# Seven half-size products of the last layer: one PSUM tile per output block, K blocks in pairs, one operand change issued later

## The chip, the cores and the metric

One core of one Trainium2 chip runs the whole program. The metric is the device time of one execution in microseconds, median over the runs. TensorE (PE) multiplies and writes only to PSUM; VectorE (DVE), ScalarE (ACT) and GpSimd (POOL) prepare its operands and read its results; SyncE (SP) issues nearly all DMAs.

## The reference

Attention over 12 heads and two batches of 448 tokens (scores capped with tanh, softmax, times v), then a gated MLP with a token-mixing matrix, then a token-mixing MLP and a channel MLP:

```python
    xt = x.transpose(0, 2, 1)
    h = np.maximum(xt @ w_tok1, 0.0) @ w_tok2
    u = x + h.transpose(0, 2, 1)
    h2 = np.maximum(u @ w_ch1, 0.0) @ w_ch2
    return (u + h2).astype(np.float32)
```

The change touches the last product alone: `relu(...) @ w_ch2`, with 1536 inner channels, 768 output channels and 2 x 448 tokens, and the sum with `u` that follows it.

## The kernel before, in words

Every product takes its two operands as a high part (fp32r) and a rest, and adds three matmuls per K block of 128: high x high, high x rest, rest x high (`three`). The high part is a cast (line 417 on ACT, 422 on POOL), the rest a subtraction (line 434 on DVE, 435 on POOL).

The program is not emitted in the order in which it is written. Each step becomes an `Op` with a key (a wish for its place), dependencies, buffers and one or more engines that may run it, each with a modelled duration and a handicap in ns. `Plan.schedule` is a list scheduler: it repeatedly takes the operation that can start first, the lower key in a tie, and writes out one fixed order per engine. Buffers are tiles with a tag and a fixed number per tag (`BUFS`): 20 of `a`, 13 of `h`, 6 of `v`, `q` and `x`, 3 of `t`; in PSUM four of `gm` (one bank each) and two of `sc` (two banks each). A `Part` is a view of a tile that the planner follows as a buffer of its own; the tile is given back when all its parts are done. `DVE` and `POOL` work on SBUF alone shares a modelled port.

The last layer, `ch2_all`, is done with seven products of half-size blocks in place of eight (a 2 x 2 scheme in which sums and differences of blocks are multiplied). Rows of the weight halves are `a11, a12, a21, a22`, the token halves `b11, b12, b21, b22`, each in six K blocks `j`. The phases, in the order of PE:

- phase 0: a11 b11 into banks `x`; copied by ACT to `part` (line 1206); phase 1 adds a12 b21 onto it, giving output rows 0 to 2 of batch 0
- phase 2: (a22 - a11 + a21) (b22 - b12 + b11) into banks `y`, in the code `s2` and `t2`
- phase 3: the changed a11 times the changed b12 into banks `z`; read by DVE to `part[3 + i]` (line 1185); phase 4 adds a22 times the changed b21 onto it
- phase 5: the changed a21 times the changed b11 into banks `v`; read by DVE onto `U`; phase 6 adds the changed a12 times b22

A phase has three output blocks `i` of 128 channels, hence 6 x 3 steps of three matmuls (`product`, line 1168 issues them). The order is set by `step`: before, in phases 0 to 5 for each `j` the blocks 0, 1, 2 one after the other; in phase 6 all `j` of block 0, then of block 1, then of block 2. `banks` hands out the three accumulators of a phase: blocks 0 and 1 are the two halves of one `sc` tile, block 2 is a `gm` tile; in phases 5 and 6 the third is `last_bank`, which lives past the end.

The operands of a step (`weight`, `tokens`) take a fresh `a` tile each. The six changes of a K block (lines 1216 to 1224) are one DVE or POOL operation each (line 1105 on DVE, 1106 on POOL): four make `s2` and `t2`, the others change a12, b21, b12 and a21 in place. `t2` and `s2` are tiles of tag `t`. `combine` with `LATE_ON` adds intermediate results to `U` outside the products. The kernel ends with a branch, the last addition (line 1383) and two stores.

Of the kernel before, what the change touches and what calls it, by code (L numbers as in the profile page):

```python
# [13 lines left out]
ALU = mybir.AluOpType  # L14
PSUM = bass.MemoryType.PSUM

B, H, S, D = 2, 12, 448, 64
# [14 lines left out]
KH = NC // 2  # L32
# [13 lines left out]
WARM = 6  # L46
ANY = {"ACT": 0, "DVE": 0, "POOL": 0}
CAST, REST_ON = ANY, {"DVE": 0}
SUM_ON, LATE_ON, HI_ON = {"DVE": 0, "POOL": 300}, {"DVE": 300, "POOL": 0}, {"ACT": 0, "POOL": 300, "DVE": 600}
ON = {  # L50
    "TH": {"ACT": 300, "POOL": 0},
    "TL": {"DVE": 0, "POOL": 0},
# [215 lines left out]
class Net:  # L268
# [841 lines left out]
    def ch2_all(self, hr, kept, k, ask):  # L1110
# [5 lines left out]

        nc, io = self.nc, self.io
        key = lambda phase, j, lead=0.0: k + (KH * phase + j) * 1.72 - lead
        step = lambda phase, j, i: key(6, (j + KH * i) / 3) if phase == 6 else key(phase, j) + 0.1 * i
        whole = [self.buf("x", [128, 4, S]) for _ in range(KH)]  # L1120
        pairs = [self.a([128, 2, 384]) for _ in range(KH // 2)]
        rows = lambda i: [Part(x, lambda ap: ap[:, i]) for x in whole]
        a11 = [self.buf("v", [128, 384]) for _ in range(KH)]
        a12 = [Part(pairs[j // 2], lambda ap, j=j: ap[:, j % 2]) for j in range(KH)]
        a21, a22 = ([self.h([128, 384]) for _ in range(KH)] for _ in range(2))
        part = rows(0)
        U = [rows(1), rows(2)]
        for b in range(B):
            for d in range(ND):
# [6 lines left out]
                    key=key((2, 5, 3, 4)[2 * b + d // 3], 0, 20) + 0.1 * d,  # L1136
                )
        b11, b12 = ([hr[j][b] for j in range(KH)] for b in range(B))
        b21, b22 = ([hr[KH + j][b] for j in range(KH)] for b in range(B))
# [6 lines left out]
        def weight(t, at):  # L1146
            w = self.a([128, 2, 384], F32R)
            self.split(384, lambda: w[:, 0], lambda: w[:, 1], lambda: t.ap, [t], [w], at, HI_ON, SUM_ON)
            return w

        def tokens(t, at):
            w = self.a([128, 2, S], F32R)
            self.split(S, lambda: w[:, 0], lambda: w[:, 1], lambda: t.ap, [t], [w], at, HI_ON, SUM_ON)
            return w

        def change(out, a, b, op, n, at):
            self.combine(n, lambda: out.ap, lambda: a.ap, lambda: b.ap, op, [a, b], [out], at, SUM_ON)

        def product(phase, banks, j, a, b, more=False):
            for i in range(3):  # L1160
                terms = self.three(
                    lambda m, i=i: a[:, m, i * 128 : (i + 1) * 128], lambda m: b[:, m], [a, b]
                )

                def fn(i=i, terms=terms):
                    for n, (term, _) in enumerate(terms):
                        l, r = term()
                        nc.tensor.matmul(  # L1168
                            banks[i].ap[:, :S],
                            l,  # L1170
                            r,
                            start=not more and (j, n) == (0, 0),
                            stop=(j, n) == (KH - 1, 2),
                            skip_group_check=more,
                        )

                self.pe(3, fn, [a, b], [banks[i]], step(phase, j, i))

        def banks(last=None):
            two = self.bank2()  # L1180
            return [Part(two, lambda ap, i=i: ap[:, i]) for i in range(2)] + [last or self.bank()]

        def onto(out, bank, other, at, size=S):
            return self.dve(
                S, lambda: nc.vector.tensor_tensor(out=out.ap, in0=bank.ap[:, :S], in1=other.ap, op=ALU.add), [bank, other], [out], key=at  # L1185
            )
# [11 lines left out]
        for j in js:  # L1198
            for n, (t, row, col) in enumerate(((a11[j], 0, 0), (a21[j], 0, 1), (a22[j], 1, 1), (a12[j], 1, 0))):
                narrow(t, row, col, j, k - AHEAD + (4 * j + n) * PACE)  # L1200
        x = banks()
        for j in js:
            product(0, x, j, weight(a11[j], key(0, j, 9)), tokens(b11[j], key(0, j, 8)))
        for i in three:
            t = part[i]
# [3 lines left out]
        for i in three:  # L1209
            z = U[0][i]  # L1210
            onto(z, x[i], z, key(2, 0))
            store(z, i, 0, key(2, 1))
        y = banks()
        for j in js:
            s2, t2 = self.buf("t", [128, 384]), self.buf("t", [128, S])
            change(a11[j], a11[j], a21[j], ALU.subtract, 384, key(2, j, 16))
            change(s2, a22[j], a11[j], ALU.subtract, 384, key(2, j, 15))
            change(b11[j], b12[j], b11[j], ALU.subtract, S, key(2, j, 16))
            change(t2, b22[j], b11[j], ALU.subtract, S, key(2, j, 15))
            product(2, y, j, weight(s2, key(2, j, 9)), tokens(t2, key(2, j, 8)))  # L1220
            change(a12[j], a12[j], s2, ALU.subtract, 384, key(2, j, 7))
            change(b21[j], b21[j], t2, ALU.subtract, S, key(2, j, 7))
            change(b12[j], b22[j], b12[j], ALU.subtract, S, key(3, j, 14))
            change(a21[j], a21[j], a22[j], ALU.add, 384, key(5, j, 14))
        for i in three:
# [10 lines left out]
        for i in three:  # L1236
# [5 lines left out]
                S, lambda u=u: u.ap, lambda u=u: u.ap, lambda i=i: part[3 + i].ap, ALU.add, [u, part[3 + i]], [u], key(5, 2), LATE_ON  # L1242
# [21 lines left out]
        for i in three:  # L1264
            u = U[1][3 + i]
            last = onto(u, v[i], u, key(6, 0, 4))
# [188 lines left out]
```

## Time and profile before

| | us |
|---|---|
| median of 3 runs | 407.14 (407.09 to 408.88) |
| the profiled execution's own time | 407.99 |
| its span, first to last instruction | 406.1 |
| PE busy | 393.4 (97%) |
| DVE busy | 303.3 (75%) |
| ACT busy | 275.5 (68%) |
| POOL busy | 70.2 (17%) |

The last layer's products run from 319.1 us to the end. Busy shares are averages over stages of different kinds; the stage that the change touches has to be read by itself. A busy PE in such a table includes matmuls that overlap, so the start-to-start distance of steps shows its pace better.

### The profile page before, as it was taken

The numbers are of one execution on the slowest core, as the hardware profiler recorded it, in microseconds if no ns is written. First come the engines' busy times: TensorE is split into PE (matmuls) and PEld (weight loads), VectorE is DVE, ScalarE is ACT, GpSimd is POOL, SyncE is SP. The second block draws the span as 40 slices with busy tenths as digits, with TensorE's granted clock in tenths as the row PEclk, the third lists the DMA queues.
The fourth block names the chain that finished last, engine by engine and source line by source line (L and its number), as shares of the span: only waits on it lengthen the run. The fifth ranks groups of instructions, "written<-read, shape, count | busy, mean of one in ns | idle before, by whom it ended". The sixth has DMA issues, their size and how long they took to land. (4 is left out here: it accounts for less than half of the span.)

```text
span 406.1 us, 5812 instructions
## 1 busy us (share of the span) xinstructions
PE 393.4 (97%) x2102; PEld 302.3 (74%) x2102; DVE 303.3 (75%) x523; ACT 275.5 (68%) x443; POOL 70.2 (17%) x71
## 2 busy tenths in 40 slices
PE   8999989999999999999999999999999999998985
PEld 4222225565558899999999998899898989988974
DVE  1799999998467869975389964255984679999941
ACT  5999999999683587364268866767978445454510
POOL 1112130100002416671001110000000011750100
PEclk9999999999999999999999999999999999999999
DMA  7965343434001014043006755545564610100121
GB/s 236 392 268 196 92 163 121 162 119 157 0 2 51 1 56 140 2 155 103 2 1 218 241 190 183 168 169 180 147 187 148 222 53 0 69 1 2 69 85 59
DMA packets 19189, 48.79 MB, mean 120 GB/s; under 512 B 2384, under 2 KB 7888, under 8 KB 19152
## 3 DMA queue, kind: packets, MB, share of 16 engines
q1 hardware_dynamic: 19008, 48.23, 35.9%
q8 instruction: 18, 0.29, 0.3%
q14 instruction: 19, 0.16, 0.1%
q10 hardware_dynamic: 144, 0.11, 0.1%
HBM read 42.83 MB, written 5.51 MB: 119 GB/s over the span
## 5 line engine op out<-in xcount | busy, mean ns | idle before, releaser
L330 PE MATMUL sc<-x,a 128*128 128x384 f32 (+2 forms) x432 | 87.7, 364 | 0.0
L330 PEld LDWEIGHTS sc<-x,a 128*128 128x128 f32 x432 | 78.8, 188 | 8.8
L1168 PE MATMUL sc<-a,a 128*128 128x448 f32 x252 | 58.1, 368 | 3.9 <-DVE x L1185 3.4
L1168 PEld LDWEIGHTS sc<-a,a 128*128 128x128 f32 x252 | 47.0, 188 | 9.5 <-ACT a L417 2.3
L472 ACT ACTIVATE r<-r 128x512 f32<-128x512 f32 (+2 forms) x64 | 40.6, 639 | 11.5 <-DMA r<-ch_in 10.7
L330 PE MATMUL gm<-a,a 128*128 128x448 f32 (+1 forms) x232 | 46.3, 356 | 0.0
L330 PEld LDWEIGHTS gm<-a,a 128*128 128x128 f32 x232 | 42.0, 188 | 2.2
L585 ACT ACTIVATE a<-a,acap 128x896 f32<-128x896 f32 x42 | 43.2, 1075 | 0.1
L576 ACT ACTIVATE a<-sc,qs 128x896 f32<-128x896 f32 x42 | 41.5, 1035 | 1.9 <-DVE a L667 0.8
L506 DVE SCALAR_TENSOR_TENSOR t<-r,t 128x512 int32<-128x512 int32 (+1 forms) x34 | 25.4, 754 | 21.9 <-ACT t L498 20.1
L435 POOL TENSOR_TENSOR a<-t,a 128x512 fp32r<-128x512 f32 x12 | 18.9, 1575 | 99.4 <-DVE a L418 78.2
L330 PE MATMUL gm<-q,a 128*128 128x448 f32 x160 | 33.0, 366 | 0.0
L605 PE MATMUL sc<-q 64*64 64x448 f32 x264 | 30.1, 553 | 2.3 <-ACT a L576 2.3
L330 PEld LDWEIGHTS gm<-q,a 128*128 128x128 f32 x160 | 30.0, 188 | 2.6
L1168 PE MATMUL gm<-a,a 128*128 128x448 f32 x126 | 31.8, 367 | 0.0
L631 PE MATMUL gm<-a,v 128*64 128x448 f32 x144 | 30.9, 548 | 0.0
L330 PE MATMUL gm<-x,a 128*128 128x448 f32 x144 | 30.5, 368 | 0.0
L330 PEld LDWEIGHTS gm<-x,a 128*128 128x128 f32 x144 | 26.7, 188 | 4.9 <-DVE v L418 1.4
L484 ACT ACTIVATE t<-r 128x512 uint16<-128x512 uint16 (+1 forms) x34 | 27.1, 801 | 2.9 <-DVE a L434 2.0
L656 DVE TENSOR_TENSOR a<-a,a 128x896 f32<-128x896 f32 (+1 forms) x24 | 26.9, 1122 | 1.9 <-ACT a L585 1.6
L498 ACT ACTIVATE t<-r 128x512 f16<-128x512 f32 (+1 forms) x34 | 27.0, 799 | 0.0
L330 PE MATMUL gm<-a,x 128*128 128x512 f32 x108 | 26.5, 397 | 0.0
(128 smaller groups left out, 577.8 us busy)
## 6 DMA issues: line engine op xcount, KB each, us to landing
r<-ch_in SPq DMA_DIRECT2D x18, 512.0 KB, 3.7
r<-ch_in SPq DMA_DIRECT2D x24, 384.0 KB, 3.6
r<-w_in_in SPq DMA_DIRECT2D x12, 512.0 KB, 5.3
q<-qk_in SPq DMA_DIRECT2D x11, 448.0 KB, 7.0
v<-va_in SPq DMA_DIRECT2D x12, 256.0 KB, 6.0
r<-w_out_in SPq DMA_DIRECT2D x6, 512.0 KB, 3.3
u<-h SPq DMA_DIRECT2D x12, 224.0 KB, 2.4
x<-u SPq DMA_DIRECT2D x12, 224.0 KB, 5.3
```

Of the source, the lines that this page charges most:

```text
L330: self.nc.tensor.matmul(view(), l, rr, start=(i + m == 0), stop=(i + m == n - 1))
L435: "POOL": ("POOL", n * 2.3 + 60, lambda: nc.gpsimd.tensor_tensor(**args()), True),
L472: lambda: nc.scalar.activation(raw[:, :, 1].bitcast(F32), raw[:, :, 1].bitcast(F32), AF.Copy, scale=2.0**-112),
L484: lambda: nc.scalar.activation(t.ap.bitcast(U16)[:, 0::2], raw.ap.rearrange("p n t -> p (n t)").bitcast(U16)[:, 1::4], AF.Copy, scale=2.0* ...
L498: lambda: nc.scalar.activation(t.ap.bitcast(F16)[:, 1::2], raw[:, :, 1].bitcast(F32), AF.Copy),
L506: lambda: nc.vector.scalar_tensor_tensor(out=t.ap.bitcast(I32), in0=raw[:, :, 1], scalar=3, in1=t.ap.bitcast(I32), op0=ALU.logical_shift_l ...
L576: lambda: nc.scalar.activation(te.ap, sc[:, 0:nn, :S], AF.Tanh, scale=self.qs),
L585: lambda: nc.scalar.activation(te.ap, te.ap, AF.Exp, scale=self.acap),
L605: nc.tensor.matmul(sc[at, h, :S], part(rows, ks), part(rows, QC), start=True, stop=True)
L631: nc.tensor.matmul(A[cols, :S], V[:, 2 * j + h], E[j][:, h], start=(j == 0 and not odd), stop=(j == 2 and odd),)
L656: "DVE": ("DVE", n / 0.96 + 70, lambda: nc.vector.tensor_tensor(**args()), True),
L1168: nc.tensor.matmul(banks[i].ap[:, :S], l, r, start=not more and (j, n) == (0, 0), stop=(j, n) == (KH - 1, 2), skip_group_check=more,)
```

## The change

`banks` now takes the first half of an `sc` tile for block 0 and a `gm` tile for each of the other two blocks (before, two blocks shared one `sc` tile). In phases 0 to 5 `step` orders K blocks in pairs: block 0 with j and j+1, block 1 with both, block 2 with both. `t2` moves from the `t` tiles to row 3 of the `x` tiles, `spare`, that nothing else uses. The change of b21 that needs `t2` gets the key of phase 4 less 16 in place of phase 2 less 7. `LATE_ON` drops DVE's handicap of 300 ns.

```diff
-SUM_ON, LATE_ON, HI_ON = {"DVE": 0, "POOL": 300}, {"DVE": 300, "POOL": 0}, {"ACT": 0, "POOL": 300, "DVE": 600}
+SUM_ON, LATE_ON, HI_ON = {"DVE": 0, "POOL": 300}, {"DVE": 0, "POOL": 0}, {"ACT": 0, "POOL": 300, "DVE": 600}
...
-        step = lambda phase, j, i: key(6, (j + KH * i) / 3) if phase == 6 else key(phase, j) + 0.1 * i
+        step = lambda phase, j, i: key(phase, (j + KH * i) / 3 if phase == 6 else j // 2 * 2 + (j % 2 + 2 * i) / 3)
...
-        part = rows(0)
+        part, spare = rows(0), rows(3)
...
-            two = self.bank2()
-            return [Part(two, lambda ap, i=i: ap[:, i]) for i in range(2)] + [last or self.bank()]
+            return [Part(self.bank2(), lambda ap: ap[:, 0]), self.bank(), last or self.bank()]
...
-            s2, t2 = self.buf("t", [128, 384]), self.buf("t", [128, S])
+            s2, t2 = self.buf("t", [128, 384]), spare[j]
...
-            change(b21[j], b21[j], t2, ALU.subtract, S, key(2, j, 7))
+            change(b21[j], b21[j], t2, ALU.subtract, S, key(4, j, 16))
```

## Rows read from the trace of the kernel before

**Rows 1.** The page: busy time, share and instructions of each engine.
```profile
PE 393.4 (97%) x2102; PEld 302.3 (74%) x2102; DVE 303.3 (75%) x523; ACT 275.5 (68%) x443; POOL 70.2 (17%) x71
```

**Rows 2.** Waits of PE: for whom, total us, times, longest us.
```profile
PE sc L1168 <- DVE x L1185: 3.4, 3, 2.0
```

**Rows 3.** Windows, phases 2 to 4: PE, PEld, DVE, ACT, POOL busy, granted clock, DMA.
```profile
342.20:353.40 11.20, 11.20 (x56) 10.16 (x55) 11.20 (x23) 5.79 (x12) 8.25 (x2) 1.00 0.17 63
353.40:364.50 11.10, 11.10 (x55) 9.93 (x53) 10.69 (x17) 5.49 (x11) 5.79 (x6) 1.00 0.00 0
364.50:377.70 13.20, 11.23 (x56) 10.27 (x56) 12.51 (x25) 5.89 (x12) 0.00 (x0) 1.00 0.01 2
```

**Rows 4.** Timeline, phase 0 to 1: start, length, instruction, tiles, count, [idle before].
```profile
328.44 1.40 PE L1168 MATMUL sc<-a,a 128*128 128x448 f32 x6
...
329.68 0.78 PE L1168 MATMUL gm<-a,a 128*128 128x448 f32 x3
329.87 0.97 ACT L1206 COPY x<-sc 128x448 f32<-128x448 f32 x2 [0.61 <-PE sc L1168]
...
330.99 1.47 PE L1168 MATMUL sc<-a,a 128*128 128x448 f32 x6 [0.53 <-ACT x L1206]
```

**Rows 5.** Timeline, phase 3 to phase 4.
```profile
363.92 0.78 PE L1168 MATMUL gm<-a,a 128*128 128x448 f32 x3
...
365.38 1.14 DVE L1185 TENSOR_TENSOR x<-sc,x 128x448 f32<-128x448 f32 x2
366.44 0.61 DVE L1185 TENSOR_TENSOR x<-gm,x 128x448 f32<-128x448 f32 x1
...
366.66 1.45 PE L1168 MATMUL sc<-a,a 128*128 128x448 f32 x6 [1.97 <-DVE x L1185]
366.97 0.61 DVE L434 TENSOR_TENSOR a<-a,a 128x448 fp32r<-128x448 f32 x1
```

**Rows 6.** Timeline, phase 5 to the last matmul.
```profile
388.02 0.77 PE L1168 MATMUL gm<-a,a 128*128 128x448 f32 x3
388.22 1.16 DVE L1185 TENSOR_TENSOR x<-sc,x 128x448 f32<-128x448 f32 x2 [0.26 <-PE sc L1168]
...
389.52 4.50 PE L1168 MATMUL sc<-a,a 128*128 128x448 f32 x21 [0.74 <-DVE x L1185]
394.05 0.62 DVE L1185 TENSOR_TENSOR x<-sc,x 128x448 f32<-128x448 f32 x1 [4.15 <-PE sc L1168]
...
394.73 3.30 PE L1168 MATMUL sc<-a,a 128*128 128x448 f32 x15 [0.72 <-DVE x L1185]
...
397.87 3.81 PE L1168 MATMUL gm<-a,a 128*128 128x448 f32 x18
```

**Rows 7.** Window of line 434 (the rests on DVE) alone.
```profile
358.20:362.80 4.60, 4.59 (x4) 1.00 0.00 0
```

**Rows 8.** Timeline of POOL and DVE in phase 3, around that window.
```profile
357.89 2.65 POOL L1106 TENSOR_TENSOR x<-x,x 128x448 f32<-128x448 f32 x2
360.49 2.00 POOL L1106 TENSOR_TENSOR last<-x 128x224 f32<-128x224 f32 x2
...
362.83 0.61 DVE L434 TENSOR_TENSOR a<-a,a 128x448 fp32r<-128x448 f32 x1
...
364.84 0.61 DVE L1105 TENSOR_TENSOR x<-x,x 128x448 f32<-128x448 f32 x1
```

**Rows 9.** Timeline, the last token operand of phase 2: cast, rest, use.
```profile
347.97 1.15 DVE L1185 TENSOR_TENSOR x<-sc,x 128x448 f32<-128x448 f32 x2
...
348.04 0.57 ACT L417 CAST a<-t 128x448 fp32r<-128x448 f32 x1 [0.88 <-PE gm L1168]
...
349.57 0.62 DVE L434 TENSOR_TENSOR a<-t,a 128x448 fp32r<-128x448 f32 x1
...
351.51 1.40 PE L1168 MATMUL sc<-a,a 128*128 128x448 f32 x6
```

**Rows 10.** A rest on POOL in phase 2, by the timeline.
```profile
344.11 4.82 POOL L435 TENSOR_TENSOR a<-v,a 128x384 fp32r<-128x384 f32 x1 [10.44 <-DVE a L434]
```

**Rows 11.** The page: the group of rests on POOL (busy us, mean ns, idle before).
```profile
L435 POOL TENSOR_TENSOR a<-t,a 128x512 fp32r<-128x512 f32 x12 | 18.9, 1575 | 99.4 <-DVE a L418 78.2
```

## The prediction

> **What bounds the kernel now.** I read the page first: PE is busy 97% of the span, so what can be had without fewer matmuls is PE's idle time, 12.7 us of 406.1 [rows 1]. The waits of PE come next: 3.4 us in three waits for line 1185, DVE's reading of the accumulators, and all of these are in the last layer [rows 2]. Then the timeline, one place at a time: the starts of PE's steps tell what a stop costs better than the idle column, which counts the last matmuls of a step to their modelled ends.
>
> In phase 0, six matmuls take 329.68 - 328.44 = 1.24 us, so a step of three takes 0.62 us [rows 4]. The last step starts at 329.68, the next could start at 330.30, and starts at 330.99: 0.69 us are lost. The reader should see whom PE waits for there. Phase 1 writes first to block 0, but ACT's two copies of blocks 0 and 1 run from 329.87 to 330.84, and PE starts 0.15 us after the second. It does not wait for the third copy, of block 2. The copies themselves start only when block 1 is done too. So two halves of one `sc` tile wait for each other both ways, though the code (`Part`) means them apart.
>
> Phase 3 to 4 is the same and worse: the last step starts at 363.92, the next could at 364.54 and starts at 366.66, 2.12 us lost [rows 5]. DVE's two readings run from 365.38 to 366.52, and PE goes on 0.14 us later, while the third reading is still running. Here DVE was late itself: it reached the first reading 0.84 us after PE could have gone on.
>
> Phase 5 to 6: next possible 388.63, start 389.52, 0.89 us lost [rows 6]. In phase 6, where a block's 18 matmuls come in a row (the last block's starts are (3.81 - 0.36) / 17 = 0.203 us apart), PE has done block 0 and the first step of block 1 (21 matmuls, to 389.52 + 21 x 0.203 = 393.78) and stops until 394.73: 0.95 us. DVE's reading of block 0 lies in this stop, 394.05 to 394.67. PE waits to write block 1 until block 0 has been read. That is the plainest of the four: nothing in the arithmetic asks for it.
>
> Sum of the four: 0.69 + 2.12 + 0.89 + 0.95 = 4.65 us.
>
> The last view is the windows. In phases 2 to 4 DVE is busy 11.20 of 11.20, 10.69 of 11.10 and 12.51 of 13.20 us, at full granted clock of PE [rows 3]. So PE bounds, with DVE close behind.
>
> **The change part by part.**
>
> A tile for each block. The wait for the other half goes at all four places. Phase 6's 0.95 us goes whole: block 1 is a `gm` tile, and DVE reads block 0 beside it, idle otherwise (4.15 us before that reading). At 5 to 6 DVE waited 0.26 us for PE, so it is in time. At 0 to 1 a copy of about 0.5 us has to fit. No work is added. What it asks for is one `gm` bank more per phase: four for `x` and `y`, so `z` takes `x`'s again. `x` is read from 347.97 on [rows 9], three readings and about 1.7 us, free by 349.7; phase 3 asks for its second bank after 353.4. About 3.7 us of cover; if it were gone PE would wait for what is left of it.
>
> K blocks in pairs. Six steps of a pair are blocks 0, 0, 1, 1, 2, 2. At a phase's end block 0 is done four steps (2.5 us) ahead in place of two, block 1 two steps ahead. At its start block 1 is asked for 1.24 us after block 0, block 2 2.5 us after. So at 0 to 1 a reading of 0.5 to 0.6 us has 2.5 us of matmuls over it, and the 0.69 us goes; at 5 to 6 the 0.89 us. At 3 to 4 the first reading ended at about 365.98 and would have to end by 364.4, 1.6 us earlier: the bank is ready 1.24 us earlier, and the planner's order follows its readiness.
>
> The price of pairs is on the operand side. The second K block of a pair is wanted two steps (1.24 us) earlier, and the first one's operand tiles are held two steps longer, so their refill starts 1.24 us later. There are 20 `a` tiles, six hold the second half of the inner layer and three a12: eleven for operands, four in a pair in work. Where the refill is all ACT and DVE wait for, the lead shrinks by up to 2.5 us. The shortest lead that I found is the last token operand of phase 2: cast at 348.04 after a wait for a tile, rest at 349.57 to 350.19, use at 351.51, 1.3 us [rows 9]. Moved up by 1.24 us, and by the 0.69 us gained before it, the use is at 349.58: 0.6 us late, 0.9 if the cast comes 1.24 - 0.69 us later and all behind it follows without a gap. Next is phase 4: the fourth token rest ends at 367.58 [rows 5]; its use is the eighth step of a phase that now starts at 363.85, so at 363.85 + 7 x 0.61 = 368.1. Half a microsecond is left even with DVE's order as it was.
>
> `t2` in spare rows and b21's change later. Six DVE operations of 0.62 us, about 0.53 us from start to start, leave the stretch ahead of phase 2's last operands and come back before phase 4's tokens. No operation is added, no DMA. The rows don't tell b21's change from the others on line 1105, but two that lay ahead of 349.57 cover the 0.6 to 0.9 us above; if POOL or a worse place in the order eats it, the 0.9 us is the cost. Also `t2` no longer shares three tiles with `s2`. b21 comes no later than phase 4's tokens, which had the lead worked out above.
>
> LATE_ON. In phase 3 POOL ran four late additions, 4.65 us [rows 8]. Beside them four rests on DVE took 362.83 - 358.21 = 4.62 us, read as 4.59 busy [rows 7]; the next four took 364.84 - 362.83 = 2.01 us [rows 8]. So these additions cost DVE 2.6 us, about the lateness of 0.84 + 1.14 at 3 to 4. On DVE they would cost two of 0.62 and two of at most 0.39, near 1.9 us, and can lie after the phase's start. Between a gain of 2.6 and a loss of 1.9 us on DVE I take a gain of about 1: some may stay on POOL while DVE reads banks. In PE's time it is part of the 2.12 us and not added.
>
> Sum on the profiled run's time: 407.99 - 4.65, plus 0.3 for remainders (a third of the 0.9 us in phase 2, bounds 0 and 0.9; at 3 to 4 between 0 and 1.6 I take none, as bank and DVE are both earlier) gives 403.6. That run is 0.85 above the median of 407.14; against the median 402.8 us. The 4.4 us from the last matmul, 397.87 + 3.81, to the span's end stay [rows 6]: last block, branch, addition, stores are not touched.
>
> **Rivals.**
>
> A, DVE is the new limit: the waits for tiles go, but DVE, full in phases 2 to 4 [rows 3], keeps its order. Then 1.6 us stay at 3 to 4 and 0.9 in phase 2: 407.14 - 4.65 + 2.5 = 405.0. For it: DVE's load. Against: operands of phases 3 to 5 had leads, DVE's load falls if anything.
>
> B, pairs give it back: PE stops at each of the nine pairs of phases 2 to 4 for a refill. At half a microsecond each, 4.5 us, the time is 407.0. Against: only one operand is late by the rows. The change not doing what it says, with waits between blocks still there, gives 407.1; against it, no third reading was waited for. Both together.
>
> C, slower: POOL takes a rest or a change that PE wants soon. One rest on POOL took 4.82 us in phase 2, beside a full DVE [rows 10], where its group has 1.575 [rows 11]: 3.2 us more. A lead such as that of phase 4's fourth token rest, used at 366.66 + 9 x 0.61 = 372.15, 4.6 us, hides it; with up to 2.5 us less it need not. Without cover each costs PE 3.2 us: two give 402.5 + 6.4 = 408.9, and from there it is slower than before by over 0.5%; three, one in each of phases 2 to 4, 412. For it: the planner does not know this hold. Against: POOL gets few such operations here, and two long ones stopped PE nowhere. The Trainium skill, SBUF — State Buffer, Who interferes with whom, says that a VectorE instruction with two SBUF inputs and a GpSimd instruction that reads SBUF exclude each other for the whole instruction. By it the four additions would have held DVE for their full 4.65 us; the trace shows 2.6, so the hold is there but partial, and I leave C small.
>
> **How the numbers follow.** Forecast 0.60, A 0.20, B 0.12, C 0.08. A measurement of this kernel can tell about 0.5%, 2.0 us, from no change: faster is below 405.1, slower above 409.2. Faster: 0.60 and three quarters of A, 0.75; same: the rest of A and B, 0.17; slower 0.08. Range: down to 401.6, all 4.65 us and another 0.9 if the 216 matmuls of phases 0 to 3 come at 0.203 in place of 0.207 us; up to 406.8, A and part of B.
>
> **What would show it.** Right: no wait of PE for lines 1185 and 1206; steps of phases 0 to 6 without a gap, and the last matmul 4 to 5 us earlier after the same start at 319.1; few late additions on POOL; no long L434 beside them. A shows as waits for line 434 ahead of phases 2 and 4, B as regular gaps every six steps, C as a wait for POOL's line 422, 435 or 1106. A changed start of phase 0 or a longer tail would put me wrong in another way.

## The result, and the profile after

The changed kernel takes 403.24 us (median of 6 runs, 402.42 to 403.85), the kernel before beside it 408.08 (407.09 to 408.88): a ratio of 0.988, 95% interval 0.986 to 0.990. Forecast were 402.8 us, 401.6 to 406.8. The profiled execution took 403.15 us against 407.99, its span 401.4 against 406.1. Of 39 later executions of the kernel before, 17 had a mean granted clock of 0.999 or 1.00 and took 407.6 us (median), 22 had 0.993 to 0.996 and took 408.8, while all six of the changed kernel had 0.999 or 1.00, so some 0.5 us of the 4.84 between the medians can be the clock and not the change.

The page of the changed kernel, busy time of each engine, answers to [rows 1]:

```profile
PE 392.6 (98%) x2102; PEld 302.5 (75%) x2102; DVE 303.3 (76%) x527; ACT 273.9 (68%) x442; POOL 59.2 (15%) x68
```

All its waits of PE; of the last layer's line 1168 none is left, where [rows 2] had 3.4 us (lines after `banks` are one lower now, 1184 for 1185):

```profile
PE sc L605 <- ACT a L576: 2.6, 3, 1.8
PE sc L409 <- DVE idle L405: 1.0, 1, 1.0
PE sc L618 <- ACT a L576: 0.7, 1, 0.7
PE gm L686 <- DVE a L656: 0.2, 1, 0.2
```

Its timeline around the end of phase 0, PE and then ACT. Answers to [rows 4]:

```profile
327.54 2.64 PE L1168 MATMUL gm<-a,a 128*128 128x448 f32 x12
330.02 1.40 PE L1168 MATMUL sc<-a,a 128*128 128x448 f32 x6
...
327.74 0.53 ACT L1205 COPY x<-sc 128x448 f32<-128x448 f32 x1
328.98 0.53 ACT L1205 COPY x<-gm 128x448 f32<-128x448 f32 x1 [0.71 <-PE gm L1168]
...
330.54 0.52 ACT L1205 COPY x<-gm 128x448 f32<-128x448 f32 x1
```

Twelve `gm` matmuls from 327.54 at 0.2067 us end where phase 1 starts, 330.02. The three copies now come 1.24 us apart and more, each behind its own block; the first two lie under phase 0's last steps, the third beside phase 1's first.

The end of phase 3, PE and DVE, for [rows 5]:

```profile
361.02 2.64 PE L1168 MATMUL gm<-a,a 128*128 128x448 f32 x12
363.50 1.40 PE L1168 MATMUL sc<-a,a 128*128 128x448 f32 x6
...
361.75 0.61 DVE L1184 TENSOR_TENSOR x<-sc,x 128x448 f32<-128x448 f32 x1
...
362.75 0.61 DVE L1184 TENSOR_TENSOR x<-gm,x 128x448 f32<-128x448 f32 x1
...
364.11 0.61 DVE L1184 TENSOR_TENSOR x<-gm,x 128x448 f32<-128x448 f32 x1
```

The first reading ends at 362.36, 1.14 us before phase 4 starts, where it ended 1.4 us after PE could have gone on; the third ends at 364.72, and block 2 is written from 363.50 + 2.48 = 365.98.

From phase 5 to the end, PE, for [rows 6]:

```profile
382.10 1.40 PE L1168 MATMUL sc<-a,a 128*128 128x448 f32 x6
383.34 2.64 PE L1168 MATMUL gm<-a,a 128*128 128x448 f32 x12
385.82 3.88 PE L1168 MATMUL sc<-a,a 128*128 128x448 f32 x18
389.54 7.60 PE L1168 MATMUL gm<-a,a 128*128 128x448 f32 x36
```

No stop. But look at the pace: the last 36 matmuls take (7.60 - 0.37) / 35 = 0.2066 us each, where the last 18 before took 0.203. Phases 0 to 6, first start to last end, take 318.86 to 397.14, 78.28 us; before, 319.14 to 401.68, 82.54 us. So 4.26 us came from here, 0.28 from an earlier start and about 0.2 from the tail, which is shorter now.

POOL's one late addition, for [rows 8], and then the busy times of PE, PEld, DVE, ACT and POOL in the stretch that held phases 2 and 3 before, for [rows 3]:

```profile
355.44 0.98 POOL L1106 TENSOR_TENSOR last<-x 128x224 f32<-128x224 f32 x1 [2.56 <-DVE x L1184]
```

```profile
342.20:364.50 22.30, 22.30 (x109) 20.26 (x108) 22.29 (x43) 10.38 (x22) 2.40 (x3) 1.00 0.08 30
```

DVE is as full as PE there, and PE waits for none of its operands.

### The profile page after: what moved, and what is told of

Same layout as the page of the kernel before. It is cut to its first block, busy times and chain, and to the rows that moved or that the text cites. A ratio compares the mean times of both kernels' runs of the same rounds, so it can differ in the third digit from the quotient of the medians.

```text
span 401.4 us, 5817 instructions
## 1 busy us (share of the span) xinstructions
PE 392.6 (98%) x2102; PEld 302.5 (75%) x2102; DVE 303.3 (76%) x527; ACT 273.9 (68%) x442; POOL 59.2 (15%) x68
## 5 line engine op out<-in xcount | busy, mean ns | idle before, releaser
L1168 PE MATMUL gm<-a,a 128*128 128x448 f32 x252 | 55.2, 368 | 0.0
L1168 PEld LDWEIGHTS gm<-a,a 128*128 128x128 f32 x252 | 47.3, 188 | 4.8
L330 PEld LDWEIGHTS gm<-a,a 128*128 128x128 f32 x232 | 42.0, 188 | 2.2
L1168 PE MATMUL sc<-a,a 128*128 128x448 f32 x126 | 29.1, 368 | 0.0
```

Of the source, the lines that this page charges most:

```text
L330: self.nc.tensor.matmul(view(), l, rr, start=(i + m == 0), stop=(i + m == n - 1))
L1168: nc.tensor.matmul(banks[i].ap[:, :S], l, r, start=not more and (j, n) == (0, 0), stop=(j, n) == (KH - 1, 2), skip_group_check=more,)
```

## Experiments

Each was timed beside the kernel before; `phases` is the first start to the last end of line 1168 (with the split's own line) in the profiled execution. The phases are the sharper measure of the two, since whole runs scatter by 1 to 2 us; but each is of one execution. The runs were timed in several rounds, so ratios compare better than medians.

| run | us, median | ratio to before, 95% | phases, us |
|---|---|---|---|
| before | 408.08 | | 82.54 |
| changed | 403.24 | 0.9862 to 0.9901 | 78.28 |
| tiles alone | 405.15 | 0.9911 to 0.9959 | 79.39 |
| pairs alone | 405.75 | 0.9941 to 0.9970 | 81.41 |
| tiles, LATE_ON | 403.77 | 0.9867 to 0.9914 | 78.64 |
| changed, shared tile | 405.89 | 0.9932 to 0.9972 | 80.48 |
| changed, t2 and b21 as before | 402.53 | 0.9850 to 0.9909 | 77.63 |
| changed, LATE_ON as before | 403.40 | 0.9863 to 0.9914 | 78.28 |
| tiles and pairs only | 403.08 | 0.9839 to 0.9876 | 78.65 |
| changed, threes | 402.90 | 0.9832 to 0.9865 | 78.63 |
| changed, one matmul split | 401.95 | 0.9828 to 0.9871 | 76.78 |
| changed, stop ahead (phases behind the added matmul) | 403.88 | 0.9882 to 0.9914 | 76.84 |
| before, one matmul split | 408.53 | 0.9981 to 1.0003 | 82.47 |

**Tiles alone.** On the kernel before:

```diff
-            two = self.bank2()
-            return [Part(two, lambda ap, i=i: ap[:, i]) for i in range(2)] + [last or self.bank()]
+            return [Part(self.bank2(), lambda ap: ap[:, 0]), self.bank(), last or self.bank()]
```

> The kernel before with one PSUM tile per output block and nothing else. Theory (PE waits for the other half of a shared tile, and at phase 3 to 4 also for DVE, which is late by itself): the stops of 0.69, 0.89 and 0.95 us at 0 to 1, 5 to 6 and in phase 6 go; at 3 to 4 the first reading still ends 1.4 us after the last step could be followed, so of 2.12 us about 1.6 stay. Gain 3.0 us, 4.6 at most. Rival (the wait is for the readings themselves, not for the tile; the pairs do the work): the stops stay, gain under 0.5 us.

Its timeline at 3 to 4, the one place where PE still stops:

```profile
364.14 0.61 DVE L1184 TENSOR_TENSOR x<-sc,x 128x448 f32<-128x448 f32 x1
364.67 1.14 DVE L1184 TENSOR_TENSOR x<-gm,x 128x448 f32<-128x448 f32 x2
...
364.90 0.84 PE L1168 MATMUL sc<-a,a 128*128 128x448 f32 x3 [1.43 <-DVE x L1184]
```

PE goes on 0.15 us after the first reading, with two more still to come. So the wait for the other half was the tile's, and it is gone here and at the other three places, whose stops are gone but for 0.1 us at 5 to 6. What is left is DVE's lateness, 1.43 us by the idle column and 1.59 by starts, where 1.6 was expected. The phases are 3.15 us shorter, 3.0 expected.

**Pairs alone.**

```diff
-        step = lambda phase, j, i: key(6, (j + KH * i) / 3) if phase == 6 else key(phase, j) + 0.1 * i
+        step = lambda phase, j, i: key(phase, (j + KH * i) / 3 if phase == 6 else j // 2 * 2 + (j % 2 + 2 * i) / 3)
```

> The kernel before with K blocks in pairs and nothing else. Theory: with block 1 done two steps (1.24 us) before a phase's end, two readings of the shared tile (1.15 us) just fit, so 0 to 1 and 5 to 6 lose 0 to 0.2 us in place of 0.69 and 0.89; the 0.95 us of phase 6 stays, its order being the same; phase 2's last operand is 0.6 to 0.9 us late, a new stop there; 3 to 4 between 0 and 2.1. Gain about 1.5 to 3 us. Rival (pairs starve PE of operands): about 0.5 us lost at each of nine pairs, no faster than before.

```profile
327.59 0.53 ACT L1206 COPY x<-sc 128x448 f32<-128x448 f32 x1 [0.62 <-PE sc L1168]
...
328.18 0.87 PE L1168 MATMUL sc<-a,a 128*128 128x448 f32 x3 [0.62 <-ACT x L1206]
```

I had the place wrong. PE stops at 327.4 to 328.2, inside phase 0, not at its end: block 0 is done four steps early, ACT copies it, and PE may not write block 1, the other half of the tile, meanwhile. At 3 to 4 the stop stays at the end:

```profile
361.94 1.37 PE L1168 MATMUL gm<-a,a 128*128 128x448 f32 x6
362.73 1.14 DVE L1185 TENSOR_TENSOR x<-sc,x 128x448 f32<-128x448 f32 x2
...
364.02 2.30 PE L1168 MATMUL sc<-a,a 128*128 128x448 f32 x10 [0.71 <-DVE x L1185]
```

PE has done block 2 and goes on only behind DVE's readings of both halves. It is so at 5 to 6 too (0.57 us by the idle column), and 0.72 us stay in phase 6. So the pairs alone removed none of the four stops; that at 3 to 4 became shorter, 0.87 us by starts in place of 2.1. The phases are 1.1 us shorter, below the 1.5 to 3 that were expected. Of the starving at every pair there was next to nothing: the last token operand of phase 2, put at 0.6 to 0.9 us, cost 0.09 us by starts.

**The changed kernel with a shared tile.** `banks` as before, all else changed.

```diff
-            return [Part(self.bank2(), lambda ap: ap[:, 0]), self.bank(), last or self.bank()]
+            two = self.bank2()
+            return [Part(two, lambda ap, i=i: ap[:, i]) for i in range(2)] + [last or self.bank()]
```

> The changed kernel with blocks 0 and 1 again in the two halves of one tile. Theory (the halves wait for each other, wherever the order puts them): inside the last pair of phases 0, 3 and 5, PE stops after the first step of block 1 until block 0 has been read, 0.6 to 0.9 us each as in the run with pairs alone, and 0.9 us in phase 6: 2.5 to 3.5 us slower than the changed kernel. Rival (pairs give the readings 2.5 us of cover, so tiles matter in phase 6 alone): 0.9 us slower.

Its waits of PE for line 1168, four in all:

```profile
PE sc L1168 <- DVE x L1185: 1.9, 3, 0.7
...
PE sc L1168 <- ACT x L1206: 0.6, 1, 0.6
```

2.2 us slower in the phases, 2.65 by the medians, where 2.5 to 3.5 were expected. By starts the four stops come to 3.5 us, and the faster pace (below), which PE has from the first stop on, gives back about 1.3. As with pairs alone, the stop lies inside the phase in phase 0 only; those of phases 3 and 5 lie at the end. The separate tiles are needed even with everything else in place.

**Tiles and the late additions.** Tiles alone, with DVE's handicap dropped:

```diff
-LATE_ON, HI_ON = {"DVE": 300, "POOL": 0}
+LATE_ON, HI_ON = {"DVE": 0, "POOL": 0}
```

> The kernel before with one tile per block and no handicap for DVE's late additions, K blocks one by one. Theory (the 1.43 us left at 3 to 4 with tiles alone is DVE held up by POOL's four additions, 2.6 us on four rests): most of these additions move to DVE behind the readings, the stop falls to 0 to 0.5 us, no L434 over 0.8 us beside them; about 1 us faster than tiles alone. Rival (DVE is late by its own load, the additions only change engine): the stop stays 1 to 1.5 us and only the pairs can remove it.

```profile
357.22 1.15 POOL L435 TENSOR_TENSOR a<-q,a 128x448 fp32r<-128x448 f32 x1
357.54 1.25 DVE L434 TENSOR_TENSOR a<-h,a 128x384 fp32r<-128x384 f32 x1
...
364.50 0.84 PE L1168 MATMUL sc<-a,a 128*128 128x448 f32 x3 [0.48 <-DVE x L1184]
```

The stop falls from 1.43 to 0.48 us, as expected. But it does not fall quite as the theory has it. Two late additions and a rest (line 435, which DVE had before) now run on POOL in this phase, and three rests of DVE beside them still take 1.0 to 1.25 us, where none over 0.8 was expected; of the two additions that moved to DVE one lies ahead of the readings. So the 0.95 us come from a shorter hold and from one rest less on DVE, against one addition more; this run does not part them.

**LATE_ON as before in the changed kernel.**

```diff
-LATE_ON, HI_ON = {"DVE": 0, "POOL": 0}
+LATE_ON, HI_ON = {"DVE": 300, "POOL": 0}
```

> The changed kernel with DVE's handicap of 300 ns for the late additions put back. Theory: POOL runs four of them in phase 3, the four rests beside them on DVE take about 4.6 in place of 2.0 us, but the first bank of phase 3 is ready 1.24 us earlier: PE stops for 0 to 1 us at 3 to 4, the same time as the changed kernel or up to 1 us slower. Rival (this handicap is what made DVE late, and it alone counts at 3 to 4): the stop of about 2 us comes back.

No stop, phases of 78.28 us as in the changed kernel. In phase 3 the planner put only two of POOL's late additions ahead of the readings, not four; two rests of DVE beside them took 1.03 and 1.08 us. With 2.5 us of cover from the pairs the first reading still ends 0.43 us before phase 4 starts. The rival fell.

**t2 and b21 as before in the changed kernel.**

```diff
-            s2, t2 = self.buf("t", [128, 384]), spare[j]
+            s2, t2 = self.buf("t", [128, 384]), self.buf("t", [128, S])
...
-            change(b21[j], b21[j], t2, ALU.subtract, S, key(4, j, 16))
+            change(b21[j], b21[j], t2, ALU.subtract, S, key(2, j, 7))
```

> The changed kernel with t2 back in the three t tiles and b21's change back at its early key. Theory: DVE reaches phase 2's last operands later, and PE stops for 0.6 to 0.9 us ahead of the last pair of phase 2 and nowhere else: 0.6 to 0.9 us slower than the changed kernel. Rival (the other edits leave enough lead): no stop, the same time as the changed kernel.

Its timeline at the end of phase 2 and the start of phase 3:

```profile
348.28 0.78 PE L1168 MATMUL sc<-a,a 128*128 128x448 f32 x3
...
348.90 1.40 PE L1168 MATMUL gm<-a,a 128*128 128x448 f32 x6
349.07 1.16 POOL L435 TENSOR_TENSOR a<-t,a 128x448 fp32r<-128x448 f32 x1
...
350.14 0.82 PE L1168 MATMUL sc<-a,a 128*128 128x448 f32 x3
350.28 0.30 PEld L1168 LDWEIGHTS sc<-a,a 128*128 128x128 f32 x2 [0.16 <-POOL a L435]
...
352.24 0.30 PEld L1168 LDWEIGHTS sc<-a,a 128*128 128x128 f32 x2 [0.23 <-DVE a L434]
```

The last token rest of phase 2 is on POOL now and ends at 350.23, 0.05 us before the weights that need it; one operand of phase 3 is 0.23 us late. So the lead is used up to nothing, which the later b21 change and the spare row prevent, but by starts PE loses 0.05 us here and 0.2 us in all, not 0.6 to 0.9. The three lines of PE show why: the planner has undone the last pair of phase 2. Block 0 gets one K block, blocks 1 and 2 get it too, and only then comes the second, 1.24 us later than in a pair, which is what the pair had taken from the lead. It does the same with pairs alone and with tiles and pairs only. And yet the phases are 0.65 us shorter than in the changed kernel. That led to the last question, the pace.

**Tiles and pairs only**, all three lesser edits undone (the diffs of the two runs above together).

> One tile per block and K blocks in pairs, without the other three edits (t2 in a t tile, b21's change early, DVE's handicap of 300 ns). Theory (these two do all the work; the other three buy lead that PE does not need): no wait for lines 1185 and 1206, two or three short stops of 0.1 to 0.3 us for rests around phase 2 to 3 as in the run without the t2 edits, which shift the pace to 202.6 ns for the rest: within 1 us of the changed kernel, rather below it. Rival (each alone is harmless but together they cost): a stop over 1 us at 3 to 4 or in phase 2.

Its waits of PE for line 1168:

```profile
PE gm L1168 <- DVE x L1184: 0.4, 1, 0.4
...
PE sc L1168 <- DVE x L1184: 0.2, 1, 0.2
```

0.6 us in two waits for readings at 3 to 4 and in phase 4, where none was expected, with five late additions on POOL in phases 3 and 4; phases of 78.65 us. By starts these waits, with the slow first matmul behind each, and two late operands of up to 0.1 us cost 1.2 us, of which the faster pace behind them gives back 0.9. So the three lesser edits do remove waits, though the time of this kernel, 403.08 us, does not set it apart from the changed one.

**Threes in place of pairs.**

```diff
-j // 2 * 2 + (j % 2 + 2 * i) / 3)
+j // 3 * 3 + (j % 3 + 3 * i) / 3)
```

> The changed kernel with K blocks in threes in place of pairs: six of the eleven operand tiles are in work and held four steps longer than one by one. Theory (the price of grouping is lead, and a pair leaves 2 to 3 us of it): with threes the next group's last operands start when the group in work gives tiles back, about 3 to 4 us before use at first and with less from group to group while DVE is full; stops of 0.3 to 1 us at several of the eight group changes of phases 1 to 4, 2 to 5 us slower than the changed kernel. Rival (the planner orders DVE well enough): no stops, the same time.

```profile
363.62 2.38 PE L1168 MATMUL sc<-a,a 128*128 128x448 f32 x9
```

Nine matmuls that take 2.02 us elsewhere take 2.38 here, a late rest of phase 4; that is all, 0.36 us, where 2 to 5 were expected. My working of the operand lead was too dark: it kept the order of DVE and POOL as it was, and the planner lays it out anew for each order of PE.

**One matmul split.** The second matmul of phase 0 is issued as two of 224 columns:

```diff
+                        if (phase, i, j, n) == (0, 0, 0, 1):
+                            for cs in (slice(0, S // 2), slice(S // 2, S)):
+                                nc.tensor.matmul(banks[i].ap[:, cs], l, r[:, cs], start=False, stop=False)
+                            continue
```

> The changed kernel with one matmul of 378 issued as two of 224 columns, the second of the first step of phase 0. On the side: in the runs so far a matmul of phases 0 to 6 starts 206.7 ns after the one before until PE has stopped once, for as little as 0.3 us, and 202.6 ns after it from there on (and once back after another stop). If any break of the even row of matmuls shifts PE from one pace to the other, the pace is 202.6 from phase 0 on and the time 378 x 0.0041 = 1.5 us shorter than the changed kernel's. If it takes a stop, nothing changes.

Its timeline at phase 0, and the last two blocks of phase 6:

```profile
319.05 0.38 PE L1170 MATMUL sc<-a,a 128*128 128x224 f32 x2
...
388.17 7.46 PE L1172 MATMUL gm<-a,a 128*128 128x448 f32 x36
```

(7.46 - 0.36) / 35 = 0.2029 us each to the end; phases of 76.78 us, 1.50 less than in the changed kernel, where 1.5 was expected. At 401.95 us (401.75 to 402.06) it is the fastest kernel of the study; it was not timed beside the changed one (its runs lie at 402.42 and above), and the two intervals of ratios overlap.

**A real stop ahead of phase 0**, in the changed kernel: one more matmul of 64 columns (two instructions in the trace) whose operand ACT writes last.

```diff
+                        if (phase, i, j, n) == (0, 0, 0, 0):
+                            nc.tensor.matmul(banks[i].ap[:, :64], self.ident, hr[-1][0].ap[:, :64], start=True, stop=True)
...
-                self.pe(3, fn, [a, b], [banks[i]], step(phase, j, i))
+                self.pe(3, fn, [a, b] + ([hr[-1][0]] if phase == 0 else []), [banks[i]], step(phase, j, i))
```

> The changed kernel with a real stop ahead of phase 0: one more matmul of 64 columns that reads the last unit of the layer before, so PE waits for ACT's 0.92 us instruction. The stop costs about 1.2 us. If a stop shifts the pace to 202.6 ns, phases 0 to 6 are 1.5 us shorter and the kernel 0.3 us faster than the changed one; if the pace has another cause (the place in the program, the engines beside), it is 1.2 us slower.

```profile
320.06 0.43 PE L1169 MATMUL sc<-a,ident 128*128 128x64 f32 x2 [1.01 <-ACT a L1098]
320.31 1.47 PE L1170 MATMUL sc<-a,a 128*128 128x448 f32 x6
...
389.70 7.45 PE L1170 MATMUL gm<-a,a 128*128 128x448 f32 x36
```

The faster pace follows the stop, 76.84 us from 320.31, so the split's own form is not needed; that it is the stop, and not the short matmul added with it, this run alone does not show. The stop costs what the pace gives: 403.88 us, no faster than the changed kernel, where 0.3 us faster was expected.

**The split in the kernel before**, the same diff.

> The kernel before with the second matmul of phase 0 issued as two halves, nothing else. Theory (the split shifts the pace whatever the order of blocks): phases 0 to 3 at 202.6 in place of 206.7 ns, 216 x 0.0041 = 0.9 us, the four stops stay at about 4.6 us: 0.6 to 0.9 us faster than the kernel before. Rival (the pace hangs on the changed order or tiles): no change. A stop in between may shift the pace back, which would show as 206.7 from that place on.

Its timeline, phase 0, the start of phase 1 and the last block:

```profile
328.57 1.38 PE L1172 MATMUL sc<-a,a 128*128 128x448 f32 x6
329.79 0.77 PE L1172 MATMUL gm<-a,a 128*128 128x448 f32 x3
331.10 1.47 PE L1172 MATMUL sc<-a,a 128*128 128x448 f32 x6 [0.54 <-ACT x L1210]
332.41 0.78 PE L1172 MATMUL gm<-a,a 128*128 128x448 f32 x3
333.03 1.40 PE L1172 MATMUL sc<-a,a 128*128 128x448 f32 x6
334.27 0.78 PE L1172 MATMUL gm<-a,a 128*128 128x448 f32 x3
...
398.03 3.88 PE L1172 MATMUL gm<-a,a 128*128 128x448 f32 x18
```

Phase 0 runs at (329.79 - 328.57) / 6 = 0.203 us; after the stop at 330.4 it is (334.27 - 333.03) / 6 = 0.207. A stop can put the pace back, and here it does. From 3 to 4 on the pace is 0.203 as in the kernel before, but behind the stop of phase 6 it is (3.88 - 0.37) / 17 = 0.206 again, where the kernel before kept 0.203. So 0.2 us are won in 54 matmuls and 0.1 lost at the end, no change that the timing shows, where 0.6 to 0.9 us were expected.

## Why the prediction was right, point by point

**The four stops.** 4.65 us by distances of starts, all gone. That they came from the shared tile was the reading of which copy PE waited for; tiles alone left next to nothing of three, and the shared tile in the changed kernel brought stops back at all four places.

**The lateness at 3 to 4.** Put at 1.6 us behind PE with DVE's order kept and none in the forecast. Tiles alone measured 1.59 us by starts (1.43 by the idle column). It has two partial cures: the late additions on DVE take it to 0.48 by that column, the pairs to 0.16, with another 0.44 for block 2 a little later (tiles and pairs only). With pairs, the t2 and b21 edits take the rest without LATE_ON (nothing is left in the run with LATE_ON as before). They are not added, as the prediction had it.

**Remainders, 0.3 us.** None came; PE has no gap at all. The 0.6 to 0.9 us for phase 2's last operand was mis-sized: without the edits that cover it, PE lost 0.05 us there by starts (0.09 with pairs alone), for the planner undid that pair. The step that failed is the one that moved PE's uses and took PE's pairs, and every other engine's order, as fixed.

**The sum.** 4.65 less 0.3 is 4.35 us; the phases gave 82.54 - 78.28 = 4.26. The closeness is in part luck, for two terms were not in the sum. Each stop also made the first matmul after it slow (in the last fence, of the same order, the six after the stop take 332.41 - 331.10 = 1.31 us to the next group's start, against 1.24 for the six after them). In the kernel before this is 0.07 to 0.11 us at each of the four, 0.27 in all beyond the 0.07 that the 0.95 us already hold. And phases 4 to 6, which ran at 0.2026 us a matmul before, run at 0.2067 now, 162 x 0.0041 = 0.66 us lost: with the stop at 3 to 4 went the faster pace that followed it. 4.65 + 0.27 - 0.66 = 4.26. The net loss of 0.39 stands by chance where the forecast had 0.3 for remainders. The start and the tail, which the prediction left as they were, gave about 0.5 us more; and the forecast of the median started from 407.14, where six runs now have 408.08.

**The rivals.** A: DVE is full, but no rest is late. B: pairs did not starve PE in the changed kernel and threes did so once, by 0.36 us; the tile was the cause. C: POOL has one late addition left and no rest (line 435) in these phases, and PE waits for nothing of it; that late additions hold DVE showed in tiles with LATE_ON. POOL's hold shows in the four long rests of the kernel before, in phase 3:

```profile
358.21 1.31 DVE L434 TENSOR_TENSOR a<-q,a 128x448 fp32r<-128x448 f32 x1
359.45 1.50 DVE L434 TENSOR_TENSOR a<-h,a 128x384 fp32r<-128x384 f32 x1
...
360.87 1.09 DVE L434 TENSOR_TENSOR a<-a,a 128x448 fp32r<-128x448 f32 x1
361.89 1.02 DVE L434 TENSOR_TENSOR a<-h,a 128x384 fp32r<-128x384 f32 x1
```

POOL's four additions end at 359.04, 360.53, 361.48 and 362.49, and each rest ends 0.42 to 0.48 us after one of them. The Trainium skill, SBUF — State Buffer, Who interferes with whom, has a VectorE instruction with two inputs in SBUF and a GpSimd instruction that reads SBUF exclude each other for a whole instruction; the ends agree with a rest that waits for the end of the addition beside it. The prediction read the rule as a hold of DVE for all 4.65 us and so called it partial at 2.6; but the rests ran in turn with the additions, so 2.6 us lost does not speak against the rule. The 1.575 us that C set against the rest of 4.82 us on POOL is a mean with one of 4.04 in it; one with DVE idle took 1.29, so the price of 3.2 us was if anything low.

## What to carry to other kernels

When PE stops at the change of a phase, look which reading it waited for: if it goes on after the reading of a neighbour in the same tile, the tile is the dependency, and separate tiles, where PSUM has the banks, cost no time here. Group K blocks so that a bank is done some steps ahead, but give each bank a tile of its own first; alone, the grouping removed none of the stops and moved one into the phase. Measure a stop by the distance of starts, and the pace on both sides of it, or a gain of one hides a loss of the other.

## What the hardware showed that I had not expected

The same matmul (448 columns, its weights loaded ahead of it) comes every 0.2067 or every 0.2026 us, with the granted clock at 1.00 in the windows of both. The pace holds for tens of microseconds and changes, if at all, at a break of the row of matmuls. Which way it turns does not follow from the length of the break, measured here by starts. It became faster after stops of 2.1 us (before), 0.8 us (pairs alone) and 0.05 us (t2 and b21 as before), and after one matmul was issued as two halves. It became slower after 0.7 us (the kernel before with the split) and after one matmul 0.07 us late (tiles with LATE_ON, start of phase 6), while the same late matmul changed nothing in tiles alone, nor did 0.36 us among threes. The stop of 0.88 us in phase 6 left it as it was in the kernel before, made it slower there with the split, and faster with pairs alone. 378 matmuls make 1.5 us of it, a third of what the change won.

The two paces and the shift at a break are shown, in one traced execution of each kernel. Whether every execution of a kernel takes the same turns is not: four executions of the kernel with t2 and b21 as before lie 1.8 us apart and only one has a trace. What in PE or its weight loads keeps the paces apart, and which break turns which way, stays open.
